# Polysketch attention and a squared-ReLU layer on one core: a hand-mixed instruction order replaced by a list schedule

## The chip, the cores and the metric

The kernel runs on one core of a Trainium2 chip. The metric is the device time of one execution in microseconds. The five engines that appear are TensorE (PE, with its weight loads listed apart as PEld), VectorE (DVE), ScalarE (ACT), GpSimd (POOL) and SyncE (SP), which here only starts transfers. Each takes its own queue of instructions in order, and waits on semaphores for the others.

## What is computed

For 4 batches of 4 heads with 1088 positions and a head size of 32, each key and query vector x is sketched twice to 8 numbers, and the outer product of the two sketches gives 64 features. Linear attention is taken over these features, and its output, 4352 tokens of 128 numbers, goes through a layer of 2048 squared-ReLU units.

```python
def phi(x):
    a = np.einsum('rd,bhsd->bhsr', S1, x)
    b = np.einsum('rd,bhsd->bhsr', S2, x)
    return np.einsum('bhsi,bhsj->bhsij', a, b).reshape(*x.shape[:-1], r * r)
q_p, k_p = (phi(q), phi(k))
kv = np.einsum('bhsf,bhsd->bhfd', k_p, v)
z = np.sum(k_p, axis=2)
num = np.einsum('bhsf,bhfd->bhsd', q_p, kv)
den = np.einsum('bhsf,bhf->bhs', q_p, z)[..., None] + 1e-06
x = (num / den), as 4352 tokens of 128
h = x @ w_in
r = np.maximum(h, 0.0)
out = (r * r) @ w_out
```

## The kernel before, in words

Tokens are taken in nine blocks of up to 512 (the last has 256). Three generators write the instructions.

`keys(b)`, line 157, makes the state of batch b. DVE transposes the keys (`kT`, L162). PE projects them with the sketch matrices (`kab_ps`, L167 and L176), DVE transposes the result back (`ab`, L184, L188), PE sums the features (`kv_ps`, L200), DVE forms the products of the two sketches in three groups (`kp`, L215), and PE multiplies them with the values (`kv_ps`, L224). Then ACT copies (`kvT`, L235), PE transposes and spreads (`st_ps`, L245, L248), and ACT and DVE build the state `kvs` (L256 to L268): numerator weights in half 0, denominator weights in half 1.

`queries(u)`, line 272, makes block u of the attention output. DVE transposes the queries (`qT`, L281). For two groups of two heads PE projects (`qab_ps`, L293, both sketches of one group, then of the other), ACT copies one sketch (`bs`, L301) and DVE multiplies it with the other (`qp`, L302). PE applies the state (`nd`, L318): first the denominators of all heads into one half of a PSUM slot, then the numerators into the other half. DVE transposes the denominators (`dT`, L329), adds the constant (`den`, L332), inverts (`rec`, L338), transposes back (`rT`, L341) and multiplies into `xT` (L345).

`moe(c0, R)`, line 355, runs the layer on one block in eight steps of 256 units. A step has two first-layer matmuls (`h_ps`, L374), a ReLU on ACT (`rl`, L382), a square on DVE (`g`, L384), and two second-layer matmuls (`o_ps`, L362), which are written `LAG` = 2 steps behind. At the end DVE transposes the output (`ot`, L392) and SP stores it (L399).

PSUM has a ring of three slots (line 55), shared by `kab_ps`, `st_ps`, `qab_ps`, `nd` and `h_ps`, and one buffer each for `o_ps` and `kv_ps`.

The order of writing is mixed by hand (line 414 on). `side()` chains the keys and queries in the order in which blocks need them; between two steps of `moe` for block m, up to three pieces of the side work for block m+1 are written, until it is used up. The tile framework then makes each engine's final order from the written order and the dependencies, and lets an instruction that is ready go ahead of one that isn't.

At the start, the two sketch matrices are loaded into `S12raw` on ACT's queue (line 87), and keys, values and queries of batch 0 on SP's (line 63). Both layers' weights are loaded on POOL's queue at once (L94, L98). DVE makes masks from the identity (`zmask`, `isum`, `spread`, L116 to L131) and the sketch constants (`S12T` to `S12q`, L137 to L150).

Of the kernel before, what the change touches and what calls it, by code (L numbers as in the profile page):

```python
# [15 lines left out]
EPS = 1e-06  # L16

@with_exitstack
def kernel(
# [24 lines left out]
    ld = ctx.enter_context(tc.tile_pool(name="ld", bufs=2))  # L44
    att = ctx.enter_context(tc.tile_pool(name="att", bufs=2))
    small = ctx.enter_context(tc.tile_pool(name="small", bufs=2))
    ffn = ctx.enter_context(tc.tile_pool(name="ffn", bufs=3))
    osb = ctx.enter_context(tc.tile_pool(name="osb", bufs=2))
    ring = ctx.enter_context(tc.tile_pool(name="ring", bufs=3, space=PSUM))
    po = ctx.enter_context(tc.tile_pool(name="po", bufs=1, space=PSUM))  # L50
    pk = ctx.enter_context(tc.tile_pool(name="pk", bufs=1, space=PSUM))

    def slot(name):

        return ring.tile([128, 2, 512], F32, tag="ring", name=name)


    T8 = KB // 4
    LEFT = KB - 4 * T8
    assert LEFT == 2  # L60
    staged = {}

    def load(b):
        kst = ld.tile([128, S], F32, tag="kst", name="kst")
        nc.sync.dma_start(
            out=kst, in_=k[b].rearrange("h (p n) d -> (h p) (n d)", p=32)
        )
        vt = ld.tile([128, H, T8 + 1, D], F32, tag="vt", name="vt")
        vb = v[b].rearrange("h (p n) d -> p h n d", p=32)
        for c in range(4):  # L70
            nc.sync.dma_start(
                out=vt[32 * c : 32 * c + 32, :, :T8, :],
                in_=vb[:, :, T8 * c : T8 * c + T8, :],
            )
        for c in range(LEFT):
            nc.sync.dma_start(
                out=vt[32 * c : 32 * c + 32, :, T8, :], in_=vb[:, :, 4 * T8 + c, :]
            )
        qst = ld.tile([128, S], F32, tag="qst", name="qst", bufs=3)
        nc.sync.dma_start(  # L80
            out=qst, in_=q[b].rearrange("h (p n) d -> (h p) (n d)", p=32)
        )
        staged[b] = (kst, vt, qst)

    S12raw = consts.tile([128, 2, D], F32)
    for s, src in enumerate((S1, S2)):
        nc.scalar.dma_start(
            out=S12raw[:, s, :],
            in_=src[None, :, :].to_broadcast([16, r, D]),
        )  # L90
    load(0)

    w_in_sb = consts.tile([128, CT, 128], BF16)
    nc.gpsimd.dma_start(  # L94
        out=w_in_sb, in_=moe_w_in.rearrange("d (ct c) -> d ct c", c=128)
    )
    w_out_sb = consts.tile([128, CT, 128], BF16)
    nc.gpsimd.dma_start(  # L98
        out=w_out_sb, in_=moe_w_out.rearrange("(ct c) d -> c ct d", c=128)
    )  # L100
# [9 lines left out]
    zeros = consts.tile([128, 128], BF16)  # L110
    nc.gpsimd.memset(zeros, 0.0)

    zmask = consts.tile([128, H, 1], F32)
    nc.vector.tensor_reduce(  # L116
        out=zmask[:, :, 0],
        in_=ident.rearrange("p (t h i) -> p h t i", t=4, h=H),
        op=ALU.add,
        axis=mybir.AxisListType.XY,  # L120
    )
    isum = consts.tile([128, r], F32)
    nc.vector.tensor_reduce(
        out=isum,
        in_=ident.rearrange("p (th i) -> p i th", i=r),
        op=ALU.add,
        axis=mybir.AxisListType.X,
    )

    spread = consts.tile([128, 2, r, r], F32)  # L130
    nc.vector.tensor_copy(  # L131
        spread, isum[:, None, :, None].to_broadcast([128, 2, r, r])
    )


# [334 lines left out]
```

## Time and profile before

| | us |
|---|---|
| median of three runs | 162.45 |
| their lowest and highest | 159.29, 164.43 |
| profiled execution | 159.84 |
| its span, first to last instruction | 158.1 |

The profile and the rows below come from the profiled execution alone. The span covers its instructions; what the execution has beyond the span lies before the first and after the last one. A busy time counts each moment once in which at least one instruction of the engine was on its way. "Idle before" or "waited for" names the instruction whose end came last before the engine went on.

### The profile page before, as it was taken

The page shows a single profiled execution, that of the slowest core. Times are in us where ns is not written, and L with a number is a line of the kernel's source. Part 1 is how long each engine was busy: PE and PEld are TensorE (multiplying, and loading weights), DVE is VectorE, ACT ScalarE, POOL GpSimd, SP SyncE. Part 2 cuts the span into 40 slices and gives each one's busy share as a digit, 9 for nine tenths or more (in the row PEclk, how much of TensorE's full clock was granted, in tenths as well). Part 3 has the DMA queues.
Part 4 walks back from the last instruction along what each step waited for, and adds up shares of the span by engine and source line. Part 5 has one row for each costly group of instructions (what it writes and reads, how often), then busy time and mean ns, then how long its engine had stood idle before and what let it go on. Part 6 is the DMA issues. An engine that isn't in the chain of part 4 may idle for free.

```text
span 158.1 us, 3355 instructions
## 1 busy us (share of the span) xinstructions
PE 123.4 (78%) x1384; PEld 53.4 (34%) x1384; DVE 111.2 (70%) x207; ACT 78.9 (50%) x99; POOL 3.2 (2%) x14
## 2 busy tenths in 40 slices
PE   0007797289899987799999878899998789999970
PEld 0003542033334433333345332333445233333540
DVE  0057818648869878788695787887947968778870
ACT  3000012064939182749391727593826277949950
POOL 7000000000000000000000000000000000000000
PEclk9999999999999999999999999999999999999998
DMA  5999959200004320300030003100300030012041
GB/s 162 209 277 301 300 157 323 100 4 0 0 2 71 85 56 4 66 0 6 0 66 4 0 0 52 18 0 4 53 13 4 2 66 4 0 21 48 0 71 33
DMA packets 25295, 10.21 MB, mean 65 GB/s; under 512 B 22080, under 2 KB 24128, under 8 KB 25280
## 3 DMA queue, kind: packets, MB, share of 16 engines
q1 hardware_dynamic: 22784, 8.92, 22.3%
q0 software_dynamic: 2208, 1.05, 5.2%
q8 instruction: 11, 0.18, 0.5%
q10 hardware_dynamic: 288, 0.03, 0.2%
q14 instruction: 4, 0.03, 0.1%
HBM read 8.81 MB, written 2.23 MB: 70 GB/s over the span
## 4 chain that ended last, share of the span: by engine, by line
PE 43%; DVE 30%; ACT 13%; DMA 5%; issue 4%; ACTq 0%; DVEq 0%
ACT rl L382 11%; PE o_ps L362 10%; PE h_ps L374 9%; DVE g L384 9%; PE nd L318 8%; PE qab_ps L293 7%; DVE kp L215 6%; DMA S12raw<-in_S_dram 5%; DVE qp L302 5%; PE kab_ps L167 4%; PE kv_ps L224 3%; DVE qT L281 2%; DVE dT L329 2%; DVE ab L184 2%; DVE rT L341 2%
## 5 line engine op out<-in xcount | busy, mean ns | idle before, releaser
L382 ACT ACTIVATE rl<-h_ps 128x1024 bf16<-128x1024 f32 (+1 forms) x72 | 66.7, 980 | 38.9 <-PE h_ps L374 35.1
L384 DVE TENSOR_TENSOR g<-rl 128x1024 bf16<-128x1024 bf16 (+1 forms) x72 | 46.1, 653 | 13.3 <-ACT rl L382 12.8
L362 PE MATMUL o_ps<-g,w_out_sb 128*128 128x512 bf16 (+1 forms) x144 | 41.6, 368 | 3.8 <-DVE g L384 3.1
L374 PE MATMUL h_ps<-xT,w_in_sb 128*128 128x512 bf16 (+1 forms) x144 | 40.7, 372 | 4.6 <-DVE xT L345 2.9
L318 PE MATMUL nd<-qp,kvs 64*32 64x256 f32 (+3 forms) x336 | 16.2, 367 | 7.2 <-DVE qp L302 7.2
L362 PEld LDWEIGHTS <-w_out_sb 128*128 128x128 bf16 x144 | 13.1, 97 | 24.1 <-issue 14.4
L374 PEld LDWEIGHTS <-w_in_sb 128*128 128x128 bf16 x144 | 12.4, 97 | 23.3 <-issue 12.2
L293 PE MATMUL qab_ps<-qT,S12q 32*64 32x256 f32 (+1 forms) x288 | 18.6, 433 | 0.0
L167 PE MATMUL kab_ps<-kT,S12k 128*32 128x256 f32 x64 | 8.8, 450 | 8.3 <-DVE S12k L141 8.3
L302 DVE TENSOR_TENSOR qp<-qab_ps,bs 128x512 f32<-128x512 f32 (+1 forms) x18 | 11.4, 645 | 4.7 <-ACT bs L301 4.7
L301 ACT COPY bs<-qab_ps 128x512 f32<-128x512 f32 (+1 forms) x18 | 9.5, 564 | 6.4 <-PE qab_ps L293 6.2
L318 PEld LDWEIGHTS nd<-qp,kvs 64*32 64x32 f32 x336 | 7.2, 109 | 15.9 <-DVE qp L302 14.2
L215 DVE TENSOR_TENSOR kp<-ab 128x1024 f32<-128x1024 f32 (+1 forms) x12 | 11.2, 944 | 0.1
L235 ACT COPY kvT<-kv_ps 128x128 f32<-128x128 f32 x4 | 1.1, 265 | 20.0 <-PE kv_ps L224 20.0
L293 PEld LDWEIGHTS qab_ps<-qT,S12q 32*64 32x64 f32 x288 | 8.6, 149 | 6.8 <-issue 3.6
L329 DVE STREAM_TRANSPOSE dT<-nd 128x512 f32<-128x512 f32 (+1 forms) x9 | 6.2, 687 | 4.0 <-PE nd L318 3.9
L224 PE MATMUL kv_ps<-kp,vt 128*32 128x64 f32 (+1 forms) x288 | 7.4, 245 | 1.0 <-DVE kp L215 0.6
L392 DVE STREAM_TRANSPOSE ot<-o_ps 128x512 f32<-128x512 f32 (+1 forms) x9 | 6.2, 687 | 2.0 <-PE o_ps L362 1.8
L167 PEld LDWEIGHTS kab_ps<-kT,S12k 128*32 128x32 f32 x64 | 2.6, 121 | 13.3 <-DVE S12k L141 8.5
L137 DVE STREAM_TRANSPOSE S12T<-S12raw 128x64 f32<-128x64 f32 x1 | 0.2, 245 | 9.7 <-DMA S12raw<-in_S_dram 9.7
L224 PEld LDWEIGHTS kv_ps<-kp,vt 128*32 128x32 f32 (+1 forms) x288 | 5.3, 123 | 5.0 <-DVE kp L215 3.6
L281 DVE STREAM_TRANSPOSE qT<-qst 128x512 f32<-128x512 f32 (+7 forms) x12 | 6.1, 536 | 0.5 <-DMA qst<-in_q_dram 0.5
(40 smaller groups left out, 48.6 us busy)
## 6 DMA issues: line engine op xcount, KB each, us to landing
kst<-in_k_dram SPq DMA_DIRECT2D x4, 544.0 KB, 5.4
qst<-in_q_dram SPq DMA_DIRECT2D x4, 544.0 KB, 6.2
vt<-in_v_dram SPq DMA_DIRECT2D x16, 128.0 KB, 4.0
out_dram<-ot SPq DMA_DIRECT2D x20, 64.0 KB, 1.9
w_in_sb<-in_moe_w_in_dram POOLq DMA_DIRECT2D x1, 512.0 KB, 8.1
w_out_sb<-in_moe_w_out_dram POOLq DMA_DIRECT2D x1, 512.0 KB, 15.7
out_dram<-ot SPq DMA_DIRECT2D x4, 56.0 KB, 1.8
out_dram<-ot SPq DMA_DIRECT2D x4, 48.0 KB, 3.5
```

The costliest lines, as they stand in the source:

```text
L167: nc.tensor.matmul(ps[32 * c : 32 * c + 32, 0, C8 * s : C8 * s + C8], S12k[:, s, :], kT[:, C8 * c : C8 * c + C8], start=True, stop=True,)
L215: nc.vector.tensor_tensor(out=kp[:P, :n].rearrange("p t h i j -> p (t h) i j"), in0=a[:, :, :, None].to_broadcast([P, n * H, r, r]), in1=b ...
L224: nc.tensor.matmul(kv_ps[32 * h : 32 * h + 32, :F], vt[:P, h, t, :], kp[:P, t - t0, h].rearrange("p i j -> p (i j)"), start=False, stop=(t ...
L293: nc.tensor.matmul(ps[F * c : F * c + F, e, 256 * s : 256 * s + W], S12q[32 * h : 32 * h + 32, s].rearrange("p i j -> p (i j)"), qT[32 * h ...
L301: nc.scalar.copy(bs[:, :, :W], ps[:, :, 256 : 256 + W])
L302: nc.vector.tensor_tensor(out=qp[:, 2 * g : 2 * g + 2, :W], in0=ps[:, :, :W], in1=bs[:, :, :W], op=ALU.mult,)
L318: nc.tensor.matmul(nd[32 * h : 32 * h + 32, c, 256 * x + w0 : 256 * x + w0 + f1 - f0], state[b][F * c : F * c + F, x, h, :], qp[F * c : F ...
L329: nc.vector.transpose(dT[:, :, :W], nd[:, :, 256 : 256 + W])
L362: nc.tensor.matmul(o_ps[:, :R], w_out_sb[:, ct, :], gs[cp][:, e, :R], start=(ct == 0), stop=(ct == CT - 1),)
L374: nc.tensor.matmul(h_ps[:, e, :R], w_in_sb[:, 2 * cp + e, :], xT[:, c0 : c0 + R], start=True, stop=True,)
L382: nc.scalar.activation(rl[:, :, :R], h_ps[:, :, :R], ACTF.Relu)
L384: nc.vector.tensor_mul(g[:, :, :R], rl[:, :, :R], rl[:, :, :R])
```

## The change

- A small planner stands in the kernel (`Op`, `Buf`, `Plan`). Each piece of work is added as an operation with an engine, a time for which it holds the engine, a latency, its dependencies, a priority, the buffers that it takes and those of which it is a last reader. `run()` plays the whole program through with these times: it picks the engine that can start soonest, takes on it the operation of lowest priority number among those that can start within 0.05 us of the first, and writes its instructions at that point.
- `tc.manual_schedule()` keeps the written order, so that each engine's queue is what the planner wrote.
- Denominators and numerators (`den_ps`, `num_ps`) take a ring slot each, where `nd` held both. In the plan the numerators' matmuls come after the reciprocal has been issued. The two `qab_ps` groups take two slots together, and their matmuls run over all four heads for the first sketch, then for the second.
- Buffers: `rl` 3 to 4, `g` 3 to 6, `ot` 2 to 3, `kp`, `kvs` and `bs` 2 to 3. The ring stays at three slots.
- Start: S1 is the first load on SP, S2 the first on ACT. The keys of each batch come in two pieces, for batch 0 one on SP and one on ACT. The weights' loads wait on POOL for the first piece of the keys (`gate`). Twelve matmuls of zeros (512 columns) stand first on PE, and `zeros` is set by DVE. The masks are an operation of low urgency with no dependency in the plan.
- In `moe` no lag is written; a step's second-layer matmuls follow the order of the plan.

```diff
--- before.py
+++ after.py
...
+    def ready(self, op):
+        t = 0.0
+        for d in op.deps:
+            if d.end is None:
+                return None
+            t = max(t, d.end)
+        for d in op.after:
+            if d.issued is None:
+                return None
+            t = max(t, d.issued)
+        for buf in op.take:
+            used, bufs = self.used[buf.pool], self.pools[buf.pool][3]
+            if len(used) >= bufs:
+                for d in used[len(used) - bufs].readers:
+                    if d.end is None:
+                        return None
+                    t = max(t, d.end)
+        return t
+
+    def run(self):
+        free, mode, left, log = {}, {}, list(self.ops), []
+        while left:
+            best = {}
+            for op in left:
+                t = self.ready(op)
+                if t is None:
+                    continue
+                for eng, (busy, lat, fn) in op.alts.items():
+                    at = max(t, free.get(eng, 0.0))
+                    best.setdefault(eng, []).append((at, op))
+            assert best, "no operation is ready"
+            eng = min(best, key=lambda e: min(a for a, _ in best[e]))
+            first = min(a for a, _ in best[eng])
+            at, op = min(
+                ((a, o) for a, o in best[eng] if a <= first + SLACK),
+                key=lambda c: (c[1].prio, c[1].index),
+            )
+            busy, lat, fn = op.alts[eng]
+            if op.mode is not None:
+                if mode.get(eng, op.mode) != op.mode:
+                    at += MODE_SWITCH
+                mode[eng] = op.mode
+            free[eng] = at + busy
+            op.issued, op.end = at + busy, at + lat
+            for buf in op.take:
+                pool, shape, dtype, _ = self.pools[buf.pool]
+                buf.tile = pool.tile(shape, dtype, tag=buf.pool, name=buf.name)
+                self.used[buf.pool].append(buf)
+            fn()
+            log.append((at, busy, eng, op))
+            left.remove(op)
+        return log
...
+SLACK = 0.05
+MODE_SWITCH = 0.1
+WARM = 12
+KP_POOL = ()
+SQ_ACT = ()
+TOGETHER = True
+K_LEAD = 18.0
+Q_LEAD = 2.0
+Q_END = 0.0
...
+    pool("kp", [128, 4, H, r, r], 3)
+    pool("kvs", [128, 2, H, D], 3)
...
+    pool("bs", [128, 2, 256], 3)
...
+    pool("rl", [128, 2, 512], 4, BF16)
+    pool("g", [128, 2, 512], 6, BF16)
+    pool("ot", [128, 512], 3)
+    pool("ring", [128, 2, 512], 3, space=PSUM)
+    pool("o", [128, 512], 1, space=PSUM)
+    pool("kv", [128, 512], 1, space=PSUM)
...
+    ctx.enter_context(tc.manual_schedule())
...
+    zeros = consts.tile([128, 512], BF16)
+    nc.vector.memset(zeros, 0.0)
     S12raw = consts.tile([128, 2, D], F32)
...
+    nc.sync.dma_start(out=S12raw[:, 0, :], in_=S1[None, :, :].to_broadcast([16, r, D]))
+    nc.scalar.dma_start(out=S12raw[:, 1, :], in_=S2[None, :, :].to_broadcast([16, r, D]))
...
+        for i, (c0, c1) in enumerate(((0, 2 * C8), (2 * C8, S))):
+            k_ops.append(dma(
+                ("SP", first)[i],
+                lambda e, c0=c0, c1=c1: e.dma_start(
+                    out=kst.tile[:, c0:c1], in_=kb[:, c0:c1]
+                ),
+                deps=deps, after=k_ops[:1], prio=prio, take=[kst] if i == 0 else [],
+            ))
...
+    load(0, -90.0, first="ACT")
+    gate = consts.tile([128, 1], F32)
+
+    def weights():
+        nc.gpsimd.tensor_copy(gate, loaded[0][0].tile[:, 2 * C8 - 1 : 2 * C8])
+        nc.gpsimd.dma_start(
+            out=w_in_sb, in_=moe_w_in.rearrange("d (ct c) -> d ct c", c=128)
+        )
+        nc.gpsimd.dma_start(
+            out=w_out_sb, in_=moe_w_out.rearrange("(ct c) d -> c ct d", c=128)
+        )
+
+    w_op = plan.add("POOL", 3.0, 8.0, weights, deps=loaded[0][1], prio=-80.0)
...
+    def warm():
+        ps = Buf("o", "warm_ps")
+        for n in range(WARM):
+            plan.add(
+                "PE", 0.43, 0.6,
+                lambda: nc.tensor.matmul(
+                    ps.tile, zeros[:, :128], zeros, start=True, stop=True
+                ),
+                prio=-100.0, take=[ps] if n == 0 else [], last=[ps], mode="full",
+            )
+
+    warm()
...
+    sk_op = plan.add("DVE", 0.8, 0.9, sketches, deps=[
+        plan.add("SP", 0.0, 3.5, lambda: None, prio=-99.0)], prio=-95.0)
...
+    mk_op = plan.add("DVE", 0.8, 0.9, masks, prio=-50.0)
...
+        def sketch(gs):
+            for s in range(2):
+                for g in gs:
+                    for e in range(2):
+                        h = 2 * g + e
+                        for c in range(2):
+                            nc.tensor.matmul(
+                                ps[g].tile[F * c : F * c + F, e, 256 * s : 256 * s + W],
+                                S12q[32 * h : 32 * h + 32, s].rearrange("p i j -> p (i j)"),
+                                qT.tile[32 * h : 32 * h + 32, W * c : W * c + W],
+                                start=True,
+                                stop=True,
+                            )
+
+        if TOGETHER:
+            op = plan.add("PE", 0.1 + 0.78 * f, 0.3 + 0.78 * f, lambda: sketch((0, 1)),
+                          deps=tr + [sk_op], prio=p(0.15), take=ps, last=[qT], mode="q")
+            sk = [op, op]
...
+        dps, nps = Buf("ring", "den_ps"), Buf("ring", "num_ps")
...
-                            nd[32 * h : 32 * h + 32, c,
-                               256 * x + w0 : 256 * x + w0 + f1 - f0],
-                            state[b][F * c : F * c + F, x, h, :],
-                            qp[F * c : F * c + F, h, w0 : w0 + f1 - f0],
+                            to.tile[32 * h : 32 * h + 32, c, w0 : w0 + f1 - f0],
+                            state[b][0].tile[F * c : F * c + F, x, h, :],
+                            qp.tile[F * c : F * c + F, h, w0 : w0 + f1 - f0],
                             start=True,
                             stop=True,
...
+        da = plan.add("PE", 0.05 + 0.42 * f, 0.28 + 0.42 * f, lambda: apply(1, dps),
+                      deps=prods + st_deps, prio=p(0.55), take=[dps], last=[qp] + kvs_last,
+                      mode="nd")
...
+        na = plan.add("PE", 0.05 + 0.42 * f, 0.28 + 0.42 * f, lambda: apply(0, nps),
+                      deps=prods + st_deps, after=[t3], prio=p(0.8), take=[nps],
+                      last=[qp] + kvs_last, mode="nd")
+        x_ready[u] = plan.add(
+            "DVE", 0.06 + 0.54 * f, 0.18 + 0.54 * f,
+            lambda: nc.vector.tensor_tensor(
+                out=xT[:, g0 : g0 + 2 * W].rearrange("p (c w) -> p c w", c=2),
+                in0=nps.tile[:, :, :W],
+                in1=rT.tile[:, :, :W],
+                op=ALU.mult,
+            ),
+            deps=[na, t4], prio=p(1.0), last=[nps, rT],
...
+            a1 = plan.add("PE", 0.432 * f, 0.432 * f + 0.2, first, deps=[x_ready[m], w_op],
+                          prio=i, take=[h], mode="full")
...
+            last = plan.add("PE", 0.432 * f, 0.432 * f + 0.2, second, deps=[a3],
+                            after=[last], prio=i, take=[o] if cp == 0 else [], last=[g],
+                            mode="full")
...
+    keys(0, (-60.0, -40.0))
     for u in range(NU):
-        before.setdefault(last_q[u] // S, u)
-
-    def side():
-
-        for u in range(NU):
-            for b, first in before.items():
-                if first == u:
-                    yield from keys(b)
-                    if b + 1 < B:
-                        load(b + 1)
-            yield from queries(u)
-            yield ("unit", u)
-
-    work = side()
-
-    def until(u):
-        for step in work:
-            if step == ("unit", u):
-                return
-
-    until(0)
-    for m in range(NU):
-        ready = m + 1 >= NU
-        for _ in moe(512 * m, min(512, N_TOK - 512 * m)):
-            for _ in range(3):
-                if not ready and next(work) == ("unit", m + 1):
-                    ready = True
-        if not ready:
-            until(m + 1)
+        if u and need[u] != need[u - 1]:
+            load(need[u], 8.0 * (u - 2) - 12.0, deps=[started[need[u] - 1], w_op])
+            keys(need[u], (8.0 * (u - 1) - K_LEAD, 8.0 * (u - 1) + 2.0))
+        queries(u, (-45.0, -20.0) if u == 0 else (8.0 * (u - 1) - Q_LEAD, 8.0 * u - 1.0 - Q_END))
+        moe(u)
+    plan.run()
```

## Rows read from the trace of the kernel before

**Rows 1.** The page, part 1: busy us of each engine, share of the span.
```profile
PE 123.4 (78%) x1384; PEld 53.4 (34%) x1384; DVE 111.2 (70%) x207; ACT 78.9 (50%) x99; POOL 3.2 (2%) x14
```
**Rows 2.** Busy time by stretch: length; PE, PEld, DVE, ACT, POOL; clock; DMA share; GB/s.
```profile
30.90:146.00 115.10, 103.56 (x1160) 43.05 (x1161) 89.75 (x161) 69.66 (x84) 0.00 (x0) 1.00 0.12 22
146.00:158.00 12.00, 7.01 (x43) 3.92 (x41) 6.19 (x14) 6.35 (x11) 0.00 (x0) 0.96 0.20 34
...
68.73:75.18 6.45, 5.98 (x29) 2.35 (x26) 5.62 (x10) 5.61 (x6) 0.00 (x0) 1.00 0.02 4
...
83.55:114.84 31.29, 27.90 (x327) 11.85 (x327) 24.52 (x45) 18.24 (x22) 0.00 (x0) 1.00 0.10 17
```
**Rows 3.** Waits in the loop, 30.9 to 146: us in total, times, longest.
```profile
ACT rl L382 <- PE h_ps L374: 35.1, 20, 7.4
...
PEld nd L318 <- DVE qp L302: 12.0, 14, 1.3
DVE g L384 <- ACT rl L382: 12.0, 29, 2.2
```
**Rows 4.** The chain of waits up to 31 us: start, us, what.
```profile
1.38 8.19 DMA S12raw<-in_S_dram
...
10.24 1.28 DVE kT L162 x2
...
12.16 1.94 PE kab_ps L167 x16
...
19.88 1.04 PE qab_ps L293 x2
...
21.49 1.94 PE qab_ps L293 x28
...
28.07 0.73 DVE dT L329
...
30.06 0.70 DVE xT L345
```
**Rows 5.** Timeline, groups of TensorE matmuls: start, us, engine, line, out<-in, count.
```profile
30.90 1.01 PE L374 MATMUL h_ps<-xT,w_in_sb 128*128 128x512 bf16 x2 [2.90 <-DVE xT L345]
31.84 2.04 PE L293 MATMUL qab_ps<-qT,S12q 32*64 32x256 f32 x32
...
63.48 0.60 PE L374 MATMUL h_ps<-xT,w_in_sb 128*128 128x512 bf16 x2
64.02 1.15 PE L293 MATMUL qab_ps<-qT,S12q 32*64 32x256 f32 x32
...
67.73 1.07 PE L318 MATMUL nd<-qp,kvs 64*32 64x256 f32 x24 [0.24 <-DVE qp L302]
...
72.01 1.03 PE L374 MATMUL h_ps<-xT,w_in_sb 128*128 128x512 bf16 x4
...
77.36 0.84 PE L167 MATMUL kab_ps<-kT,S12k 128*32 128x256 f32 x10
...
82.89 0.65 PE L224 MATMUL kv_ps<-kp,vt 128*32 128x64 f32 x32
```
**Rows 6.** Timeline, the second query block of the loop's `nd` slot and ACT's wait.
```profile
56.98 0.65 PE L318 MATMUL nd<-qp,kvs 64*32 64x64 f32 x12
...
61.02 1.02 ACT L382 ACTIVATE rl<-h_ps 128x1024 bf16<-128x1024 f32 x1 [1.79 <-DVE dT L329]
...
62.74 0.68 DVE L345 TENSOR_TENSOR xT<-nd,rT 128x512 bf16<-128x512 f32 x1
```
**Rows 7.** Loads at the start: S12raw's landing times, the weights', the queries' first wait.
```profile
DMA to landing us min/median/max: 4.3/6.3/8.2
...
w_in_sb<-in_moe_w_in_dram POOLq DMA_DIRECT2D x1, 512.0 KB, 8.1
w_out_sb<-in_moe_w_out_dram POOLq DMA_DIRECT2D x1, 512.0 KB, 15.7
...
12.76 0.71 DVE L281 STREAM_TRANSPOSE qT<-qst 128x512 f32<-128x512 f32 x1 [0.52 <-DMA qst<-in_q_dram]
```

More of the change, by code (lines that the diff above doesn't have):

```diff
@@ L43 @@
     consts = ctx.enter_context(tc.tile_pool(name="consts", bufs=1))
[L44 to L50, printed above, removed]
@@ L51, with pool @@
[L51 to L55 removed]
+    pools, tiles = {}, {}
+    def pool(name, shape, bufs, dtype=F32, space=None):
+        if space is None:
+            p = ctx.enter_context(tc.tile_pool(name=name, bufs=bufs))
+        else:
+            p = ctx.enter_context(tc.tile_pool(name=name, bufs=bufs, space=space))
+        pools[name] = (p, shape, dtype, bufs)
     T8 = KB // 4
@@ L59 @@
     LEFT = KB - 4 * T8
+    C8 = 32 * T8
     assert LEFT == 2
[L61 to L83, printed above, removed]
@@ L85 @@
-    S12raw = consts.tile([128, 2, D], F32)
[L86 to L100, printed above, removed]
+    pool("kst", [128, S], 2)
@@ new lines, in keys @@
+            last = plan.add("PE", 0.12 * n, 0.12 * n + 0.25, accumulate,
+                            deps=[pd] + v_ops, after=[last], prio=p(0.3 + 0.2 * x),
+                            last=[kp, vt], mode="k")
+            steps.append(last)
+        kvT, zd, st = Buf("kvT", "kvT"), Buf("zd", "zd"), Buf("ring", "st_ps")
+        zj, zc, kvs = Buf("zj", "zj"), Buf("zc", "zc"), Buf("kvs", "kvs")
+        d1 = plan.add(
+            "DVE", 0.1, 0.22,
+            lambda: nc.vector.tensor_tensor(
+                out=zd.tile,
+                in0=kv.tile[:, F : F + H * r].rearrange("p (h j) -> p h j", h=H),
+                in1=zmask.to_broadcast([128, H, r]),
+                op=ALU.mult,
+            ),
+            deps=[zsum, mk_op], prio=p(0.76), take=[zd], last=[kv],
+        )
@@ new lines, in keys, with turn @@
+        c1 = plan.add(
+            "ACT", 0.2, 0.3,
+            lambda: nc.scalar.copy(
+                kvT.tile, kv.tile[:, None, :F].to_broadcast([128, 2, F])
+            ),
+            deps=steps, prio=p(0.75), take=[kvT], last=[kv],
+        )
+        def turn():
+            nc.tensor.matmul(
+                st.tile[:, 1, : H * r],
+                spread.rearrange("p c i j -> p (c i j)"),
+                zd.tile.rearrange("p h j -> p (h j)"),
+                start=True,
+                stop=True,
+            )
+            nc.tensor.transpose(
+                st.tile[:, 0, :128], kvT.tile.rearrange("p c f -> p (c f)"), ident
+            )
@@ new lines, in keys @@
+        c2 = plan.add(
+            "ACT", 0.2, 0.3,
+            lambda: nc.scalar.copy(
+                kvs.tile[:, 0].rearrange("p h d -> p (h d)"), st.tile[:, 0, :128]
+            ),
+            deps=[tn], prio=p(0.85), take=[kvs], last=[st],
+        )
+        d3 = plan.add(
+            "DVE", 0.1, 0.22,
+            lambda: nc.vector.tensor_reduce(
+                out=zc.tile[:, :, 0], in_=zj.tile, op=ALU.add, axis=mybir.AxisListType.X
+            ),
+            deps=[d2], prio=p(0.9), take=[zc], last=[zj],
+        )
@@ L309, in queries @@
-        nd = slot("nd")
-        for x in (1, 0):
+            tr.append(plan.add(
+                "DVE", 0.1 + n / 940.0, 0.22 + n / 940.0,
+                lambda c0=c0, b=b, s0=s0, n=n: nc.vector.transpose(
+                    qT.tile[:, c0 - g0 : c0 - g0 + n], loaded[b][4].tile[:, s0 : s0 + n]
+                ),
+                deps=[loaded[b][5]], after=tr[:1], prio=p(0.0), take=[qT] if not tr else [],
+                last=[loaded[b][4]],
+            ))
+            c0 += n
+        ps = [Buf("ring", "qab_ps") for _ in range(2)]
```

568 lines of the change are left out of this document (339 added, 229 removed).

## The prediction

> **What bounds the kernel now.** I read the page's busy shares first: PE 78%, DVE 70%, ACT 50% [rows 1]. No engine is full, so the time is lost between engines, and an average over the whole span cannot say where. The second view is therefore the busy time by stretch [rows 2]. It splits the 158.1 us into three stages: A, from the start to the first first-layer matmul (`h_ps`) at 30.9; B, the loop from 30.9 to 146; C, the last half block from 146 to the end. B, which is 115.1 us long, has DVE at work for 89.75 (78%) and ACT for 69.66 (61%). PE is given as 103.56 busy, but a matmul's record includes its time in the pipeline, so I count PE's work by itself below.
>
> The third view is the list of waits in B [rows 3]. ACT waits 35.1 us for `h_ps`, DVE 12.0 us for `rl`, and the weight loads of `nd` 12.0 us for `qp`: one waits for the other in a ring. ACT is starved although it is the emptiest of the three, because PE takes its queue in order and stands at `nd`, or is working through a block of `kab_ps`, `qab_ps` or `nd`, when ACT wants the next `h_ps`. The stretch from 68.73 to 75.18, with few side matmuls, shows the reverse: ACT 5.61 of 6.45 [rows 2]. The side work is thus uneven along the loop; the chain shifts from PE to DVE and ACT and back.
>
> The fourth view is the chain of waits through A [rows 4]. It begins with 8.19 us of the sketches' load, which lands at 9.57. Then one thing follows another: key transposes, two mask reductions, projection, products, `kv_ps`, and only then the query projection, in two pieces of 1.04 and 1.94 us around `st_ps`, and the `nd` matmuls.
>
> **The loop (B).** The change leaves the arithmetic as it is, apart from which instruction goes first and where `nd` lives. So what an engine must do in B stays. A period of the old loop is two blocks of 512 tokens with one batch of keys: 31.29 us, of which DVE works 24.5 [rows 2]. PE's own work in a period, from the groups of one shape [rows 5]: four `h_ps` matmuls take 1.03 and two take 0.60, so one more costs 0.215 us; 64 of the large ones are 13.8. `qab_ps` 2 x 1.15 = 2.3; `nd` 1.07 for 24 of a block's 32, so 2 x 1.45 = 2.9; `kv_ps` 2 x 0.65 and a shorter third group, 1.6; its 18 sums, at that pace, 0.4; `kab_ps` 0.84 for ten of 24 instructions of which eight are short, so about 1.3; `st_ps` some 0.8, about what three large ones take. Sum 23.1 us. ACT has 18.24. A perfect order would be bounded by DVE at 24.5, with PE close behind.
>
> How close does a fixed order come? The old loop keeps DVE at 24.52/31.29 = 78% [rows 2]; its best stretch, 68.73 to 75.18, has 5.62/6.45 = 87%. The new order lets operations of later blocks fill gaps by priority, with more buffers (`rl` 4, `g` 6, `kp` 3, `kvs` 3), so I take 90%, a little above that best stretch. PE at 23.1/27.2 = 85% then still has room, though not much, which is why I don't take 95%. B becomes 89.75/0.90 = 99.7 us, 15.4 less. Bounds: 82%, 109.5 us (5.6 less), and 97%, 92.5 us (22.6 less).
>
> The separate slots for denominator and numerator are inside this figure. Now `nd` holds one of the three ring slots from its first matmul at 56.98 to the end of `xT` at 63.42, 6.4 us, because the numerator sits there while the denominator is transposed, inverted and transposed back; ACT's `rl` waited 1.79 us for `dT` there [rows 6]. With two slots each is held for its own matmuls and one DVE instruction, about 0.6 + 0.7 + some queueing = 1.5 to 2 us. That gives back some 3 slot-us per block, worth between nothing (where the ring isn't what is late) and one such wait in every second block, 7 us in all; I count no extra, since the 90% holds it. Against it, both query groups now take two slots together. Doing the first sketch half of all four heads before the second puts neighbours on other rows of the array. One block costs 1.15 us for 32 instructions [rows 5]; it may fall to about half, or cost 0.1 more for the lost overlap with ACT's copy; PE isn't the bound, so I take zero. New waits: the numerator's matmuls now stand behind the reciprocal in plan order. Behind them on PE stand `h_ps` and `o_ps` matmuls, and ACT waits for those; the price is one DVE chain of some 0.5 us per block at worst, 4 us in all, which lies within the bounds of B.
>
> **The start (A).** Step by step, from the old chain [rows 4] and loads [rows 7]:
> - The sketches: S1 is now first on SP, S2 first on ACT, both issued at about 0.75. The two old transfers took 4.3 and 8.2 us, so S12raw lands between 5.1 and 9.0; I take 6.0, nearer the faster, because both weight loads (512 KB each) now wait for the keys. Cost: the keys' first half moves behind S1 on SP, the second behind S2 on ACT. When the keys landed before, the rows don't show (DVE was held by S12raw); at the pace of the faster sketch, 4.3 us, they come at about 5.5 to 6.
> - The masks leave the path: from the end of the key transposes at 11.52 to the projection at 12.16 are 0.64 us, now spent while DVE waits for the sketches. They need `ident` from POOL, whose whole work is 3.2 us [rows 1].
> - So the key transposes start at about 6.2 instead of 10.24, the projection at 7.6, `ab` at 9.5, the three products end at 13 with the queries' transposes among them.
> - The queries' load is issued after the values' six, as before, and its first transpose waited for it until 12.76 [rows 7]. It becomes the limit here: without the weights in front I take 12.0; bounds 11 and 14, the latter if the next batch's loads, which SP issues straight behind, share the engines. Then `qT` 1.3, `qab_ps` 1.2 to 2.0, `bs` 0.6, two `qp` 1.3, the first `nd` 0.65 to 1.1, and `dT` to `xT` 2.7 (28.07 to 30.76): 7.75 to 9.0, so the first `h_ps` at about 20.7. The state `kvs` is ready before: `kv_ps` 13.5, then `kvT`, `st_ps`, `zj` to `kvs` some 2.5, so 16.
> A goes from 30.9 to 20.7: 10.2 us less. Bounds 18 and 25. The first-layer weights took 8.1 us, the second-layer ones 15.7 [rows 7]. Issued at 6 they land at 14.1 and 21.7; the first `o_ps` is due about 2.3 us after the first `h_ps` (0.60 + 1.02, and `g` as long as `xT`, 0.68), at 23. That margin is 1.3 us; if `w_out_sb` is later than that, each us of it costs one.
>
> On the sketches the row says: their two DMAs had ACT's queue to themselves and the second still took 8.2 us while SP's loads and the weights were under way [rows 7]. The Trainium skill (DMA: Bandwidth & Descriptors, "Issuing engines are not separate DMA queues") says that transfers from any issuing engine interleave on the same 16 DMA engines, so that issuing from another engine saves only issue time. This speaks against half the step: S2 still shares with the keys. By the rule it lands at up to 9.0 and A ends nearer 22.5 than 20.7; by the faster row it lands at 5.1.
>
> PE's first matmuls ran at half pace: `qab_ps` 2.04 us at 31.84 against 1.15 at 64.02, the first pair of `h_ps` 1.01 against 0.60 [rows 5]. The granted clock of these stretches is recorded as 1.00, the 2.4 GHz level [rows 2], so that column doesn't show what the durations do. PE had stood idle through `dT` to `xT` before that pair [rows 4]. The twelve warm-up matmuls aim at this. If they hold, `kab_ps`, `qab_ps` and `nd` in A cost half; if the pause after them undoes it, they cost nothing (PE is idle then anyway). I have taken the middle. The Trainium skill (TensorE: Matmul & The Clock Gate, "HAM oscillation") says that an idle gap puts the array back on the low rate. By it A is nearer 22; by a warm array nearer 19.5.
>
> **The end (C).** Half a block with no side work: 12.0 us with DVE 6.19 and ACT 6.35 busy [rows 2]. Its latencies stay; I take 12.0, bounds 10.5 and 13.
>
> Sum against the profiled execution: 20.7 + 99.7 + 12.0 = 132.4, plus 1.7 outside the span (159.84 less 158.1) = 134.1 us. The median of the runs shown, 162.45, is 1.6% above that execution; I add 1%, **135.5 us**.
>
> **Rivals.**
> - *The loop packs almost fully* (DVE 97%, A 18.5): 18.5 + 92.5 + 12 + 1.7 = 124.7. For: three engines, none over 78%. Against: PE would be at 23.1 of 25.3 per period.
> - *The start stays late*: S2 shares the engines with the keys and the array is slow: A 25, total 138.4, with 1% 140. For: the 8.2 us row. Against: 1 MB of weights has left that interval.
> - *The loop doesn't change*: the old order already interleaves side work with the large matmuls, and waits only move. Only A gains: 159.84 - 10.2 = 149.6, about 150. Against: the stretches with ACT 61% and DVE 78% busy [rows 2].
> - *Nothing on balance*: the loop unchanged and A only 2 to 4 us better, or the change's order undone by real waits: 156 to 162.
> - *The other side: the lag is lost.* The old loop writes `o_ps` two steps behind `h_ps` by hand (LAG). The new plan has no such rule; where an `o_ps` stands ahead of the next `h_ps` on PE's queue, the step runs as a serial chain: 0.60 + 1.02 + 0.68 + 0.60 = 2.9 us [rows 5, 6], against 115.1/64 = 1.80 per step now and 1.56 forecast (eight blocks of eight). It decides where B loses what A gained plus 2%: 115.1 + 10.2 + 3.2 = 128.5 us, 2.01 per step, so if 34% of the steps are serial. With 40%: 64 x 2.10 = 134, total 20.7 + 134 + 13.7 = 168. For: plan times that are wrong by a few tenths can put it there. Against: three ring slots leave room for `h_ps` to be ready first.
>
> **How the numbers follow.** Forecast 0.52; packed loop 0.12; late start 0.14; loop unchanged 0.09; nothing on balance 0.06; lag lost 0.07. The first four are faster by over 2%, about what a measurement of this kernel can tell from no change: 0.87; within 2% 0.06; slower 0.07. The range runs from the packed loop to the unchanged one, which the bounds of B, with A at 18 and 25, also give: 18 + 92.5 + 13.7 = 124 to 25 + 109.5 + 13.7 = 148. I give 125 to 150; what lies outside is the last two cases and some of the edges, under 2 in 10.
>
> **What would show it.** Right: first `h_ps` near 20.7; S12raw no longer at the head of the chain for 8 us; a period near 27 us with DVE about 90% busy; ACT's wait for `h_ps` well under 35 us; no `rl` waiting for `dT`. Wrong: a period above 30 us; PE waiting at `o_ps` for `g` in most steps (lag lost); the first `o_ps` waiting for `w_out_sb`; the first `h_ps` after 25 us.

## The result and the profile after

The changed kernel takes 127.09 us (median of four, 126.07 to 128.53) against 161.66 us for the kernel before beside it: a ratio of 0.792, interval 0.778 to 0.806. Ratio and interval leave out executions over 1.5% above the fastest of their kernel (here one of the four after and two of the four before), so the ratio is not the quotient of the two medians, 0.786. The profile is of the slowest of the four, 128.53 us, with a span of 126.7.

The page's part 1, and the clock among its 40 slices, beside [rows 1]:

```profile
PE 110.2 (87%) x1378; PEld 50.5 (40%) x1396; DVE 105.1 (83%) x208; ACT 78.6 (62%) x99; POOL 3.3 (3%) x14
...
PEclk9999555557999999999999999999999999999998
```

Busy times hardly fell (DVE 111.2 to 105.1, ACT 78.9 to 78.6); the same work stands closer together. The clock row now has a stretch at half rate. For the kernel before nothing can be said of it: the first clock record in its trace stands at 34.2 us, and what its rows print ahead of that, 1.00, is not a measurement.

Busy time by stretch of the kernel after, columns as in [rows 2]. The loop is cut here at the first half-size `h_ps`, which in the kernel before stands at 147.54:

```profile
0.00:25.13 25.13, 17.41 (x242) 7.77 (x243) 14.09 (x33) 3.96 (x7) 3.26 (x14) 0.76 1.05 239
25.13:116.35 91.22, 87.53 (x1100) 39.35 (x1119) 85.66 (x165) 69.77 (x84) 0.00 (x0) 0.97 0.20 42
116.35:126.70 10.35, 5.30 (x37) 3.38 (x35) 5.37 (x12) 4.87 (x9) 0.00 (x0) 0.95 0.25 40
```

The start went from 30.90 to 25.13, the loop from 116.64 to 91.22 and the end from 10.56 to 10.35: 5.8 + 25.4 + 0.2 = 31.4 us of span. DVE is now at work for 94% of the loop.

The waits in the loop of the kernel after, beside [rows 3]:

```profile
ACT rl L673 <- PE h_ps L664: 12.6, 20, 2.0
...
ACT rl L673 <- remote: 6.0, 1, 6.0
...
DVE g L682 <- ACT rl L673: 2.6, 6, 0.9
```

The 6.0 us of "remote" are the wait of the first `rl`, whose releaser this trace doesn't show; in the kernel before the same wait, 7.4 us, is inside the 35.1 for `h_ps`. So ACT's 27.7 us for `h_ps` behind that first wait became 12.6 (with it, 35.1 became 18.6), DVE's 12.0 for `rl` became 2.6, and nothing above 2 us is left of the 12.0 for `qp`.

The chain of waits through the start, beside [rows 4]:

```profile
5.23 5.55 DMA qst<-in_q_dram
...
17.12 2.01 PE qab_ps L542 x32
19.13 1.12 PE den_ps L595 x16
...
21.71 1.23 PE den_ps L595 x12
...
23.37 0.90 PE num_ps L595 x12
...
24.29 0.70 DVE xT L640
```

It no longer begins with the sketches: they landed 2.1 and 2.4 us after their issue, first in line. It begins with the queries. Then comes the new order's own price: the `qab_ps` of 17.12 belongs to block 1 and stands on PE ahead of block 0's denominators, and block 1's denominators (21.71) stand ahead of block 0's numerators. Both ran at the low rate, as this row of the windows says:

```profile
16.00:28.00 12.00, 8.65 (x107) 3.58 (x108) 8.14 (x20) 2.36 (x4) 0.00 (x0) 0.50 1.06 240
```

A granted clock of 0.50 is the 1.2 GHz level. By the trace's clock record it fell at 13.1 us, and PE had been idle for most of 8.2 to 11.5; it rose at 30.1, when the first layer ran.

### The profile page after: what moved, and what is told of

The parts are those of the page before. It is cut to its first block, busy times and chain, and to the rows that moved or that the text cites. A ratio compares the mean times of both kernels' runs of the same rounds, so it can differ in the third digit from the quotient of the medians.

```text
span 126.7 us, 3355 instructions
## 1 busy us (share of the span) xinstructions
PE 110.2 (87%) x1378; PEld 50.5 (40%) x1396; DVE 105.1 (83%) x208; ACT 78.6 (62%) x99; POOL 3.3 (3%) x14
## 4 chain that ended last, share of the span: by engine, by line
PE 53%; DVE 25%; ACT 7%; DMA 4%; issue 3%; SPq 3%; DVEq 0%; ACTq 0%
PE o_ps L692 17%; PE h_ps L664 16%; DVE g L682 7%; ACT rl L673 7%; PE qab_ps L542 7%; DVE kp L412 4%; DMA qst<-in_q_dram 4%; PE num_ps L595 4%; PE kv_ps L430 4%; PE den_ps L595 3%; DVE qp L573 3%; DVE qT L527 3%; DVE ot L702 2%; PE kab_ps L348 2%; SPq L237 1%
## 5 line engine op out<-in xcount | busy, mean ns | idle before, releaser
L673 ACT ACTIVATE rl<-h_ps 128x1024 bf16<-128x1024 f32 (+1 forms) x72 | 66.5, 980 | 21.8 <-PE h_ps L664 12.6
L692 PE MATMUL o_ps<-g,w_out_sb 128*128 128x512 bf16 (+1 forms) x137 | 37.4, 371 | 1.9 <-DVE g L682 1.2
L664 PE MATMUL h_ps<-xT,w_in_sb 128*128 128x512 bf16 (+1 forms) x133 | 37.3, 373 | 1.8 <-DVE xT L640 0.9
L664 PEld LDWEIGHTS <-w_in_sb 128*128 128x128 bf16 x144 | 12.9, 98 | 18.6 <-issue 6.8
L692 PEld LDWEIGHTS <-w_out_sb 128*128 128x128 bf16 x144 | 13.1, 98 | 17.6 <-issue 7.7
L542 PE MATMUL qab_ps<-qT,S12q 32*64 32x256 f32 (+1 forms) x288 | 12.4, 405 | 3.5 <-DVE qT L527 2.1
L412 DVE TENSOR_TENSOR kp<-ab 128x1024 f32<-128x1024 f32 (+1 forms) x12 | 10.8, 921 | 0.0
L595 PE MATMUL den_ps<-qp,kvs 64*32 64x256 f32 (+3 forms) x168 | 7.3, 391 | 1.7 <-DVE den L615 1.5
L610 DVE STREAM_TRANSPOSE dT<-den_ps 128x512 f32<-128x512 f32 (+1 forms) x9 | 6.1, 675 | 2.7 <-PE den_ps L595 2.7
L337 DVE STREAM_TRANSPOSE kT<-kst 128x512 f32<-128x512 f32 (+1 forms) x8 | 5.7, 728 | 1.6 <-DMA kst<-in_k_dram 1.6
L595 PE MATMUL num_ps<-qp,kvs 64*32 64x256 f32 (+3 forms) x168 | 6.9, 369 | 0.0
L640 DVE TENSOR_TENSOR xT<-num_ps,rT 128x512 bf16<-128x512 f32 (+1 forms) x9 | 5.8, 647 | 0.6 <-PE num_ps L595 0.6
L277 PE MATMUL warm_ps<-zeros 128*128 128x512 bf16 x12 | 5.2, 623 | 1.2 <-DVE zeros L190 1.2
L629 DVE STREAM_TRANSPOSE rT<-rec 128x512 f32<-128x512 f32 (+1 forms) x9 | 6.1, 674 | 0.1
## 6 DMA issues: line engine op xcount, KB each, us to landing
w_out_sb<-in_moe_w_out_dram POOLq DMA_DIRECT2D x1, 512.0 KB, 18.8
```

The lines of the kernel that those rows point to most:

```text
L412: eng.tensor_tensor(out=kp.tile[:P, :n].rearrange("p t h i j -> p (t h) i j"), in0=a[:, :, :, None].to_broadcast([P, n * H, r, r]), in1=bb ...
L542: nc.tensor.matmul(ps[g].tile[F * c : F * c + F, e, 256 * s : 256 * s + W], S12q[32 * h : 32 * h + 32, s].rearrange("p i j -> p (i j)"), q ...
L595: nc.tensor.matmul(to.tile[32 * h : 32 * h + 32, c, w0 : w0 + f1 - f0], state[b][0].tile[F * c : F * c + F, x, h, :], qp.tile[F * c : F * ...
L664: nc.tensor.matmul(h.tile[:, e, :R], w_in_sb[:, 2 * cp + e, :], xT[:, c0 : c0 + R], start=True, stop=True,)
L673: lambda h=h, rl=rl: nc.scalar.activation(rl.tile[:, :, :R], h.tile[:, :, :R], ACTF.Relu),
L692: nc.tensor.matmul(o.tile[:, :R], w_out_sb[:, ct, :], g.tile[:, e, :R], start=(ct == 0), stop=(ct == CT - 1),)
```

## The experiments

Each kernel is the changed one with one edit, unless it says otherwise. All ratios are to the kernel before on the same chip; those without an interval are of the medians. Three columns cut the profiled span at the first `h_ps` and the first half-size `h_ps`.

| kernel | median us | ratio | start | loop | end |
|---|---|---|---|---|---|
| before | 161.66 | 1 | 30.90 | 116.64 | 10.56 |
| after | 127.09 | 0.792 (0.778 to 0.806) | 25.13 | 91.22 | 10.35 |
| framework orders again | 133.59 | 0.831 | 30.16 | 91.28 | 10.36 |
| side work bunched | 128.86 | 0.802 | 25.20 | 91.66 | 10.84 |
| one slot | 139.69 | 0.870 (0.863 to 0.877) | 24.67 | 103.20 | 10.23 |
| key products on POOL | 134.83 | 0.839 | 23.91 | 98.25 | 10.34 |
| before, two slots | 159.92 | 0.994 (0.989 to 0.999) | 31.04 | 117.18 | 11.08 |
| old buffers | 126.59 | 0.791 (0.785 to 0.796) | 23.71 | 90.41 | 10.48 |
| groups apart | 131.64 | 0.821 (0.814 to 0.829) | 25.53 | 95.89 | 10.38 |
| old loads | 128.54 | 0.803 (0.798 to 0.808) | 29.88 | 86.52 | 10.40 |
| order only | 139.29 | 0.868 (0.863 to 0.874) | 27.57 | 98.25 | 10.98 |
| seven squares on ACT | 129.74 | 0.808 (0.804 to 0.811) | 23.19 | 93.34 | 10.37 |
| start mended | 128.08 | 0.798 (0.796 to 0.801) | 21.44 | 94.41 | 10.35 |
| start mended, values once | 127.16 | 0.793 (0.788 to 0.798) | 19.31 | 95.00 | 10.39 |

My theory at this point: the order spreads the side work so that DVE, the bound, stays full; slots, grouping and buffers add little. Rivals: the slots carry it; PE is the bound; the written order matters but not that it is kept.

**Does it matter that the order is kept?**

```diff
-    ctx.enter_context(tc.manual_schedule())
```

> The planner stays and writes in the same order, with its buffers, slots and loads, but the line that keeps the written order is gone, so the framework orders each engine's queue again. If the fixed order is what packs the loop, the loop from the first full h_ps to the first half-size one grows from 91 us by at least a third of what it gained (116 before), 135 us or more in all. Rival: the gain comes from the mixing, buffers and loads, and the framework makes as good an order of it: 126 to 130 us.

133.59 us (131.26 to 134.40), 6.5 us more than after by the medians, 5.2 by the lowest of each. But the loop took 91.28 against 91.22, and of the 5.1 us between the two profiled spans 5.0 stand in the start. So the first branch is wrong in its place and the rival wrong in its time. Left to itself the framework made an equally good loop out of the planned written order; at the start it let block 1's work and the next batch's key transposes in between block 0's steps on DVE. `xT` of block 0 came at 29.42 for 24.29.

**Is it the spreading?**

```diff
-            keys(need[u], (8.0 * (u - 1) - K_LEAD, 8.0 * (u - 1) + 2.0))
+            keys(need[u], (8.0 * (u - 1) - 2.0, 8.0 * (u - 1)))
-        queries(u, (-45.0, -20.0) if u == 0 else (8.0 * (u - 1) - Q_LEAD, 8.0 * u - 1.0 - Q_END))
+        queries(u, (-45.0, -20.0) if u == 0 else (8.0 * (u - 1), 8.0 * (u - 1) + 2.0))
```

> Only priorities change: the side work for block m+1 (keys and queries) is made urgent in the first two of the eight steps of block m, as the old kernel wrote it, and no longer spread over the block and ahead of it. If the spreading fills DVE, its busy share in the loop falls from 94% towards the old 78% and the time rises to 133 to 142 us. Rival (slots, buffers or the loads made the gain): within 2% of 127 us.

128.86 us by the median, 126.75 at the lowest (after: 126.07), loop 91.66: no difference that can be told. But the edit didn't bring the old order back, so it doesn't test the spreading. In four blocks of the kernel before, DVE's queue has six squares in a row with no side work between them, and the later ones wait for `rl`:

```profile
71.92 1.28 DVE L384 TENSOR_TENSOR g<-rl 128x1024 bf16<-128x1024 bf16 x2
73.48 0.69 DVE L384 TENSOR_TENSOR g<-rl 128x1024 bf16<-128x1024 bf16 x1 [0.28 <-ACT rl L382]
...
76.34 0.69 DVE L384 TENSOR_TENSOR g<-rl 128x1024 bf16<-128x1024 bf16 x1 [0.34 <-ACT rl L382]
```

In the bunched kernel this happens once, in the last block with side work; elsewhere at most four squares stand in a row (after: three), and DVE is still at work for 94% of the loop. The planner takes what can start first and looks at priorities only within 0.05 us, so bunched priorities still gave a spread queue. The priorities don't make the gain; whether the spreading does stays open.

**The slots, in the new order and in the old.**

```diff
-        dps, nps = Buf("ring", "den_ps"), Buf("ring", "num_ps")
+        dps = nps = Buf("ring", "nd")
...
-            deps=[da], prio=p(0.6), take=[dT], last=[dps],
+            deps=[da], prio=p(0.6), take=[dT],
```

> Denominators and numerators share one ring slot again, which is held until xT is written. My theory says that the ring is not what is late: 127 to 130 us, and the waits of rl for a matmul grow by a few us at most. Rival: the separate slots carry the loop's gain, since a slot is held some 5 us per block instead of 2: 133 us or more.

139.69 us: 12.6 more, all of it in the loop. The rival stands and my zero is wrong. In one block the slot was held from 73.05 to 79.86, 6.8 us. The loop's waits show who pays; after has 12.6 and 1.8 us in the places of these rows of the one-slot kernel:

```profile
ACT rl L674 <- PE h_ps L665: 19.2, 17, 3.4
...
PEld qab_ps L542 <- ACT rl L674: 6.8, 12, 0.7
```

`qab_ps`, which needs two slots at a time, waits for `rl` to give them back. The same edit by itself, in the old kernel:

```diff
-        nd = slot("nd")
+        dps = slot("den_ps")
...
+        nps = slot("num_ps")
+        apply(0, nps)
```

> The old kernel with one edit: denominators and numerators in a ring slot each, the numerators' matmuls written after the reciprocal. In the new kernel one shared slot cost 12 us in the loop. If the slot's hold is what is late in any order, the old loop of 116.6 us falls by 8 to 12 us, 149 to 153 in all. Rival: in the hand-mixed order other waits (PE's blocks of side work) are late and the slots give 0 to 3 us: 157 to 161.

0.994 of the kernel before, at most 1.1%: the rival. In the old order the slots are worth almost nothing; the part is worth something only together with the order.

**Buffers and grouping.**

```diff
-    pool("rl", [128, 2, 512], 4, BF16)
-    pool("g", [128, 2, 512], 6, BF16)
+    pool("rl", [128, 2, 512], 3, BF16)
+    pool("g", [128, 2, 512], 3, BF16)
```

and likewise `kp`, `kvs`, `bs` and `ot` to 2.

> The new kernel with the old buffer counts (rl 3, g 3, kp, kvs and bs 2, ot 2); the plan is made with these. If the extra buffers let PE and ACT run ahead, 131 us or more, with PE or ACT waiting for g and rl to come free. Rival: the old counts are enough for a planned order: 126 to 129 us.

126.59 us: no difference. The old counts are enough, and DVE's and ACT's queues hold the same instructions in the same order as in the changed kernel. So this profile is a second one of that order: first `h_ps` at 23.71 for 25.13, loop 90.41 for 91.22, and the low clock from 16.9 to 27.2 us for 13.1 to 30.1. A start can thus differ by 1.4 us between executions of one order.

```diff
-TOGETHER = True
+TOGETHER = False
```

> The new kernel with the two query groups projected one after the other, each in its own slot taken when it is due. I counted the grouping at zero: 126 to 129 us. If the eight array tiles side by side save PE's time, 130 us or more; if two slots held together cost, 123 to 126.

131.64 us, 4.5 more, and the loop 4.7 longer. The timeline of the kernel with the groups apart, two groups of one block, and then that of the kernel after, one block:

```profile
65.68 1.09 PE L542 MATMUL qab_ps<-qT,S12q 32*64 32x256 f32 x16
68.89 1.09 PE L542 MATMUL qab_ps<-qT,S12q 32*64 32x256 f32 x16
```

```profile
50.82 1.12 PE L542 MATMUL qab_ps<-qT,S12q 32*64 32x256 f32 x32
```

Sixteen instructions of one group take 1.09 us, the thirty-two of both 1.12: the grouping saves nearly 1.1 us of PE a block. My zero rested on the row of 1.15 for 32 in [rows 5]. That was a block of the old kernel in which the framework had mixed the two groups by itself; in its blocks with keys the sixteen of one group took 1.09.

**What bounds the loop?**

```diff
-KP_POOL = ()
+KP_POOL = ((1, 0), (1, 1), (2, 0), (2, 1), (3, 0), (3, 1))
```

> Six of the twelve key products (the large ones of batches 1 to 3, 1.18 us each on DVE) go to POOL, 6 to 7 us of DVE work less. If DVE bounds the loop (94% busy), 121 to 124 us. If PE does (97% by its record), 126 to 128 us. If POOL's products come late or slow down DVE beside them, over 128 us.

134.83 us, the last branch. The timeline shows why:

```profile
28.01 4.32 POOL L412 TENSOR_TENSOR kp<-ab 128x1024 f32<-128x1024 f32 x2 [19.51 <-DVE ab L369]
29.05 1.47 DVE L682 TENSOR_TENSOR g<-rl 128x1024 bf16<-128x1024 bf16 x1 [0.47 <-ACT rl L673]
30.44 2.17 DVE L412 TENSOR_TENSOR kp<-ab 64x256 f32<-64x256 f32 x1
32.53 0.68 DVE L682 TENSOR_TENSOR g<-rl 128x1024 bf16<-128x1024 bf16 x1
```

Beside POOL's products a square took 1.47 us instead of 0.68 and a small product 2.17 instead of 0.41; each ended 0.3 to 0.6 us after a product of POOL (these two ended at 29.97 and 32.33). DVE's work in the loop rose to 88.88 us. So this run can't tell the bound. The next moves work to ACT:

```diff
-SQ_ACT = ()
+SQ_ACT = (10, 18, 26, 34, 42, 50, 58)
```

> Seven of the 72 squares go from DVE (0.67 us each, some 0.6 in a row) to ACT (about 1 us each), 4 us of DVE work less and 7 us of ACT work more. If DVE's work is what sets the end, 123 to 125 us. If PE does, 126.5 to 128. If ACT, which is 62% busy, comes late with rl, over 128.

129.74 us, 2% above. DVE's work in the loop fell to 83.21 us, ACT's rose to 76.07 of 93.34, and the loop didn't get shorter. But here ACT came in the way. The chain that ended last, from part 4 of the page, first of after and then of this run:

```profile
PE 53%; DVE 25%; ACT 7%; DMA 4%; issue 3%; SPq 3%; DVEq 0%; ACTq 0%
```

```profile
PE 32%; DVE 32%; ACT 15%; issue 5%; another core or an unknown queue 5%; DMA 4%; SPq 3%; DVEq 0%; ACTq 0%
```

ACT's share doubled, as the last branch has it, so neither run shows what less work on DVE alone would give. For PE there is the run with the groups apart: PE's record in the loop rose from 87.53 us to 94.34 (to compare with 88.86 in the old-buffers run, which has as many records), PE's share of the chain to 71%, and the loop grew by 4.7 us. More work on PE reaches the end. That less on DVE wouldn't isn't shown.

**The start.**

```diff
-    nc.sync.dma_start(out=S12raw[:, 0, :], in_=S1[None, :, :].to_broadcast([16, r, D]))
+    nc.scalar.dma_start(out=S12raw[:, 0, :], in_=S1[None, :, :].to_broadcast([16, r, D]))
...
-        nc.gpsimd.tensor_copy(gate, loaded[0][0].tile[:, 2 * C8 - 1 : 2 * C8])
```

> The new kernel with both sketches on ACT's queue, keys whole on SP first, and the weights' loads started at once. If the loads' order made the start earlier, S12raw lands after 7 us again and the first h_ps comes 2 to 5 us later than 25.1, 129 to 132 us. Rival: the queries' load and PE's low clock set the start, and nothing moves: within 1 us of 127.

The sketches landed at 6.6, the first `h_ps` came at 29.88, 4.75 us later, and the loop took 86.52, 4.7 less. The span is 126.8 for 126.7; by the median of four, 1.4 us are lost, less than the two intervals tell apart. Of the expectation the later `h_ps` came true, with sketches that landed somewhat sooner than 7 us, and the end hardly moved. While the first layer waits, the engines do keys and queries of later blocks: DVE had 16.88 us of work behind it at the first `h_ps`, against 14.09.

The other way round, three edits that bring the first layer forward:

```diff
+                          deps=tr + [sk_op], after=da_of[:1] if u == 1 else (),
+                      deps=prods + st_deps, after=na_of[:1] if u == 1 else (),
+            deps=deps, prio=prio - (0.5 if b == 0 else 0.0), take=[qst],
-WARM = 12
+WARM = 44
```

> The start mended: the queries of batch 0 are loaded ahead of the values, the projection and denominators of block 1 stand behind the denominators and numerators of block 0 on PE, and more zero matmuls (44) fill PE's pauses in the plan up to the first layer. If PE's low clock and this order made the first h_ps late, it comes at 20 to 22 us instead of 25.1. If the end follows the first h_ps, 123 to 125 us in all; if, as the run with the old loads suggests, a later first h_ps is paid back by side work done ahead, the loop grows by what the start gains and the time stays at 126 to 128.

First `h_ps` at 21.44, with a recorded clock of 1.00 up to there; the time stays, 128.08. `xT` was ready at 19.3, but zero matmuls and block 1's projection were ahead of the first layer, and then PE stood for the second layer's weights:

```profile
25.84 0.82 PE L696 MATMUL o_ps<-g,w_out_sb 128*128 128x512 bf16 x2 [1.74 <-DMA w_out_sb<-in_moe_w_out_dram]
```

The last run took that away too:

```diff
-    pool("vt", [128, H, T8 + 1, D], 2)
+    pool("vt", [128, H, T8 + 1, D], 1)
-WARM = 44
+WARM = 35
```

> The mended start with one change more: the values have one buffer instead of two, so that SP's loads of the next batches stop at the values of batch 1 until kv_ps of batch 0 is done, and nine fewer zero matmuls. In the run before this one the first second-layer matmul waited for w_out_sb until 25.8 and ACT stood 4 us. If the next batches' loads kept w_out_sb back, it now lands before 22, the first h_ps comes at 19 to 21, the 4 us hole goes, and the whole is 122 to 125 us, below the new kernel's 127.1. Rival: what the start gains the loop gives back, since PE's work in the loop is the same: 126 to 128.

`h_ps` came at 19.31 and `o_ps` no longer waited for the weights, but for `g`. The loop took 95.00, and the median is 127.16: the rival. Of 5.8 us at the start 3.8 came back in the loop (of 4.4 all of it, 4.6, against the second profile of the same order), and no difference in the time can be told from the changed kernel. Only part of this is work that had been done ahead: DVE has 88.20 us in this loop for 85.66. The rest is waiting: PE's record leaves 6.6 us of this loop idle, and 3.7 of the loop of after.

**The order alone.** These parts are undone: one `nd` slot with the numerators written right behind the denominators, groups apart, old buffers, old loads, no warm-up. The keys in two pieces, the masks off the path and the missing lag stay as in the change.

```diff
-                      deps=prods + st_deps, after=[t3], prio=p(0.8), take=[nps],
+                      deps=prods + st_deps, prio=p(0.55),
...
-WARM = 12
+WARM = 0
```

> Only the planned, kept order is left of the change: one nd slot with the numerators written right behind the denominators, groups projected one after the other, old buffer counts, old loads, no warm-up. If the parts add up as they did when taken away singly (12.6 for the slot, 4.5 for the grouping, 1.4 for the loads, nothing for the buffers), 145 to 148 us, so that the order by itself is worth 13 to 16 us. Rival: the order is worth little without the slots and the grouping, since those make the room in which it can choose: 153 us or more. Second rival: the slot's 12.6 us came only from numerators being planned late while they held a slot: 132 to 142 us.

139.29 us, 0.868: the planned order, with those three, gives 21 of the 34 us. That is better than the parts' sum, as the second rival has it: part of the one-slot loss would then come from the late numerators. One slot with early numerators and nothing else undone wasn't run, so this is argued. Undoing the rest costs 139.29 - 127.09 = 12.2 us; the grouping (4.5) and the loads (1.4) leave some 6 for the slots, an estimate that takes these parts as adding up, which no run shows. Which property of the order makes the loop shorter stays open: it isn't that the order is kept, nor the priorities, nor the buffers.

## Why the prediction was right, and where not

The direction and the range held; 127.1 stands near the lower end of 125 to 150. The likeliest value, 135.5, was 8 us too long, and its terms were wrong both ways. Against the profiled execution, 128.53, the start was 4.4 us longer than forecast, loop and end 10.1 shorter, and the added 1% (1.4) wasn't there. That the first two went opposite ways was luck: the forecast start with the measured loop, end and 1.8 outside the span would add up to 124.1, below the range.

- **The start.** 25.13 for 20.7, 4.4 too late and just beyond the upper bound of 25; 3.0 in the second profile of the same order. The steps up to the queries were better than I said: sketches by 3.23 for 6.0, key transposes at 5.60 for 6.2, queries at 10.8 for 12.0. What failed was the sequel: I put block 0's steps one behind the other, while the fixed order sets block 1's projection and denominators ahead of block 0's on PE, at the low clock, where I had taken the middle of the two levels. The denominators began at 19.1 us where my steps give 16.4 to 17.2, and from there to `h_ps` it took 6.0 for 3.4 to 3.8. PE's clock fell to 0.50 at 13.1 us, so the twelve matmuls didn't hold it; with 44 of them and two more edits it stayed at 1.00 past the first `h_ps`. The Trainium skill (TensorE: Matmul & The Clock Gate, "HAM oscillation") speaks of idle gaps undoing the rate. The trace agrees so far as PE had idled before the fall.
- **The sketches' rule.** I feared that S2, sharing the engines with the keys, might land at 9.0. It landed 2.4 us after its issue at the latest. The rule of the Trainium skill on issuing engines (DMA: Bandwidth & Descriptors, "Issuing engines are not separate DMA queues") isn't contradicted, since both sketches were issued ahead of everything else; with the old loads they took up to 5.2.
- **The loop and the end.** 99.7 + 12.0 = 111.7 predicted, 91.22 + 10.35 = 101.6 measured, less than even the rival that packs almost fully had (92.5 + 12.0). The step that was mis-sized is "what an engine must do stays": I took DVE's busy time as its work and filled it to 90%. It was filled to 94%, and the busy time itself fell to 85.66 from 90.73. The instructions didn't get shorter (their durations one by one add up to 95.9 us for 96.5); more of them overlap. So DVE's 24.5 us a period, which I called a bound, wasn't one. From `xT` of block 0 to that of block 6 two blocks took 27.2, 23.8 and 21.5 us, 24.2 in the mean, against 27 forecast and 31.7 in the kernel before.
- **Zeros that weren't.** The grouping was sized at zero and is worth 4.5 us; the slots were counted inside the 90% and are worth, with this order, 12.6 us when the numerators stay late, and some 6 by the estimate above. Both fell because I took PE and the ring as having room. PE has the largest part, 53%, of the chain that ended last.
- **Two terms that aren't independent.** I added what the start gains to what the loop gains. Three runs moved the first `h_ps` by 4.75 later and 3.7 and 5.8 earlier, and the loop gave back 4.7, 3.2 and 3.8. Against the second profile of the same order these are 6.2 later, 2.3 and 4.4 earlier, and 3.9, 4.0 and 4.6 back. So the start's term could be wrong by 4 us with little harm to the time, and was.
- **Rivals and signs.** "Lag lost" didn't come: `o_ps` waited for `g` four times, 0.9 us in all. The sketches don't head the chain, and no `rl` waited for `dT`, as the signs of being right have it; the first `h_ps` after 25 us, a sign of being wrong, came. The margin that I gave `w_out_sb` (landing at 21.7, needed at 23) was gone, as it landed at 6.9 + 18.8 = 25.7, but the late start hid it; it came to light when the start was mended.

## What to carry to other kernels

Where no engine is full and each waits for another, start from the written order, not from buffers: here it gave 21 of 34 us, and the extra buffers nothing. Test the parts in the new order and in the old one: a second slot worth up to 12.6 us in the one was worth 1 in the other. When an edit is meant to undo one property, read from the trace whether it did; the bunched priorities left the queue spread. And before shortening a start, ask what the waiting engines do meanwhile: here three changed starts left the time within 1.5 us.

## What the runs showed of the hardware that I had not expected

- Beside a float32 product on POOL (the two shown took 2.0 and 2.4 us), DVE's instructions with two inputs in SBUF didn't merely slow down: they ended shortly after POOL's (a square 1.47 for 0.68 us, a small product 2.17 for 0.41). So did one with a single input, `den`, beside a later product (1.19 for 0.17). The Trainium skill (SBUF — State Buffer, "Terms") describes a port pair shared by DVE and GpSimd that one holds for its whole instruction; the rows agree.
- Sixteen 32-row matmul instructions on two heads took 1.09 us, thirty-two on four heads 1.12.
- The rows of before print a clock of 1.00 while matmuls ran at half pace. The first clock record stands at 34.2 us there and at 21.9 in the order-only kernel, which has no warm-up either; after, with the warm-up, it stands at 6.2. Ahead of the first record only durations tell.
- In two executions of one order the low clock lasted from 13.1 to 30.1 us and from 16.9 to 27.2.
